# DeltaNet and mixture of depths on one core: the state's chain ahead in the plan, W's second copy in W's own form, a smaller first G, five elimination steps by columns

## The chip, the core and the metric

The kernel runs on one core of one Trainium2 chip. The metric is the time of one execution on the device in microseconds; three runs of the kernel before gave 325.86 us in the median (323.55 to 333.23).

## What is computed

Four batches, eight heads, 768 tokens, 48 channels a head. First a delta rule over the tokens, one state of 48x48 for each batch and head:

```python
k_n = k / (norm(k) + 1e-6)
for t in range(S):
    y[:, :, t] = einsum('bhd,bhde->bhe', q[:, :, t], state)
    v_old = einsum('bhde,bhd->bhe', state, k_n[:, :, t])
    state = state + beta_t * einsum('bhd,bhe->bhde', k_n[:, :, t], v_t - v_old)
```

Then, with x the heads' outputs side by side (4, 768, 384), a mixture of depths: each token's score is x times w_gate; the 128 tokens of the highest score in each batch go through `relu(x @ w1) @ w2` (384 to 1024 to 384), scaled by the sigmoid of the score, and are added to x; the other tokens keep x.

## The kernel before

**Chunks, blocks and the state.** The tokens are cut in chunks of 64 (`C`), 12 for each of two groups of two batches, so `NU` is 24 chunks, called i. Four chunks make a block e (`BC`), six in all. In a chunk the delta rule is a triangular system, which is solved ahead of the recurrence for all heads and halves of 32 tokens at once:

- `prep(i)` loads k and q, transposes them on PE (`turn`, L401; copies at L414), makes G, the products of k with k (`products`, L460; the first block by `first_products`, L450, in pieces of 32 rows; copy at L466), and the products of q with k (L460; masked by DVE at L473). From block 1 on, G goes to DRAM (`spill`, L470) and comes back turned (`turn_in`, L535), so that each partition holds one 32x32 matrix.
- `eliminate(e)` inverts those matrices on DVE, one per partition: the diagonal (L541), its root on ACT (L545), the scales (L549 to L554), the scaling (L570), then the steps j = 1 to 30. A step is a product of a column with a row into `tmp` (L593), the next row by itself (L579), and an addition (L599); the last steps go row by row (L579). `final` is L604. In blocks 2 to 4 (`over`) the table is then written to DRAM (`out_a`, L611) and read back turned (`back`, L617) as `tt`; in the other blocks DVE turns it (L607), and `tt` is read from `g`. `join` makes Z (L681) of the two halves.
- `recur(i)` is the recurrence. In order: R, keys times the old state (`mm_r`, L735), copied on ACT (L745); W, the table times the values (`mm_w`: L766, or L772 where `direct`), with a second copy of its lower half in another bank (L779); W's copy on ACT (L795 or L798 and L800); M, which joins the halves (`mm_m`, L790); its copy to `wbd` (L805); S, the product that adds to the state in PSUM (`mm_s`, L816); its copies (L823). The state's chain is R, W, M, S and their copies. Off it lie Q and P, the outputs (`mm_q` L833, `mm_p` L845, copy L851), the score (DVE, L863), and the values' scaling for the next chunk (`vh`, L709), which waits for the copy of R, as both use a bank.
- `ranking(g)` counts for each token the scores above its own (L939 to L980), and `depths(b)` takes the chosen tokens by an indirect DMA, runs the two layers (L1067, L1083) and writes the rows back.

**What sets the order.** Nothing is looped on the chip: `Plan` orders all operations on the host. Each has an engine, a cost, dependences, a latency, a priority (smaller goes first) and the rings of buffers it takes and gives. `pick` takes, for an engine that is free, the operations that can start earliest, and among these the smallest priority; one that would delay a `hard` one by more than 0.2 is left out unless its priority is as small. Where PE would wait in the plan, `fill` puts matmuls of constants (`filler`, L305). So costs and priorities act on the chip through the order alone: each engine, and SP's queue of DMAs, then runs its list in order.

```python
u = 10 * i            # recur: all of the chain, Q and P at u + 3
u = 40 * e - 100 + i % BC   # prep: keys and G of block e
u = 10 * i - 30       # join: Z
```

Priorities in prep for q's transposes are 10i - 20, and for the products of q with k 10i - 14.

**PSUM.** Eight banks: two pairs (`pair`), two single ones (`one`), two for the state (`psta`). `constants` writes the banks once by matmuls on ones (L341), of each pair only the second bank.

Of the kernel before, what the change touches and what calls it, by code (L numbers as in the profile page):

```python
# [16 lines left out]
C = 64  # L17
HC = 32
# [139 lines left out]
def kernel(  # L158
# [47 lines left out]
    def ring(name, count, shape, dt=FP32):  # L206
        rings[name] = [sbuf(f"{name}{m}", shape, dt) for m in range(count)]
        plan.ring(name, count)
# [23 lines left out]
    ring("zt", 3, [GI, HC])  # L232
    ring("tt", 2, [NB, C])
    ring("x", 2, [2, DM])
# [88 lines left out]
    def constants():  # L323
# [4 lines left out]
        for t in rings["q"] + rings["k"][BC:]:  # L328
            nc.gpsimd.memset(t[:, :, D:], 0.0)
        for t in rings["tt"]:  # L330
            nc.gpsimd.memset(t, 0.0)
# [7 lines left out]

        for t in [*psta, *[t[:, 1] for t in rings["pair"]]]:  # L340
            nc.tensor.matmul(t, lhsT=warm[:, :P], rhs=warm, start=True, stop=True)  # L341
# [77 lines left out]
    def prep(i):  # L419
# [21 lines left out]
        def first_products():  # L441
            kt, ps = got("kt", i), banks(kb)
            for x in range(GI):
                h4, par = divmod(x, 2)
                for bb, rt in four:
                    k_of = kt[half[rt], bb * 2 + h4]
                    for out, rows, tok, cols in ((slice(0, C), hi[bb], hi[par], half[par]),
                                                 (slice(HC, C), lo[bb], lo[par], lo[par]),
                                                 (slice(0, HC), lo[bb], lo[par], hi[par])):
                        nc.tensor.matmul(ps[rows, rt, x, out], lhsT=k_of[:, tok],  # L450
                                         rhs=k_of[:, cols], start=True, stop=True)
# [54 lines left out]
        if first:  # L506
            n["g"] = pe(1.0, first_products, n["ek"], u, take=gt, work=1024, hard=True)
            n["eg"] = [act(0.59, out_g, [n["g"]], u, give=[kb], hard=True)]
        else:
            n["g"] = pe(0.52, products("kt", kb), [*n["ek"], N[e * BC].get("g")], u, take=gt,  # L510
                        work=1024, lat=LATE["g"])
            n["eg"] = [act(0.48, out_g, [n["g"]], u, give=[kb])]
            n["sg"] = sp(0.6, spill, n["eg"], u, take=[("gd", e)] * (i % BC == 0), lat=4.6)
            n["sg"].own = 4.2
        v = 10 * i - 14
        n["w"] = pe(0.58, products("qt", kw), n["eq"] + n["ek"] + [N.get(("end", 0))], v,
                    work=1024, take=[kw, ("p", i)], lat=LATE["p"])
        n["ep"] = [dve(0.62, out_p, [n["w"]], v - 200, give=[kw])]

    def eliminate(e):  # L520
# [23 lines left out]
        def root():  # L544
            nc.scalar.activation(nrm[:, 0], nrm[:, 0], AF.Sqrt)  # L545

        def scales():
            nn, b = nrm[:, 1], bh[e % 2]
            nc.vector.tensor_scalar(out=nn, in0=nrm[:, 0], scalar1=1e-6, scalar2=-1.0,  # L549
                                    op0=ALU.add, op1=ALU.mult)  # L550
            nc.vector.reciprocal(b, nn)
            nc.vector.scalar_tensor_tensor(out=b, in0=b, scalar=-1.0, in1=b,
                                           op0=ALU.mult, op1=ALU.mult)
            nc.vector.tensor_tensor(out=b, in0=b, in1=bt[:, e], op=ALU.mult)  # L554

# [19 lines left out]
        def row(i, j):  # L575
            a = got("a", e)
            to, of = (a[:, :j, i], a[:, :j, j]) if over else (a[:, i, :j], a[:, j, :j])
            by = a[:, j, i:i + 1] if over else a[:, i, j:j + 1]
            nc.vector.scalar_tensor_tensor(out=to, in0=of, scalar=by, in1=to,  # L579
                                           op0=ALU.mult, op1=ALU.add)  # L580
# [47 lines left out]
        s["in"] = dve(0.2, diag, [ti, N.get(("nrm", e - 1)), N.get(("late", e - 1))], u, **hard)  # L628
        s["rt"] = act(0.25, root, [s["in"]], u - 1, hard=True)
        s["sc"] = dve(1.0, scales, [s["rt"], *N["beta", e]], u, **hard)  # L630
        N["nrm", e] = s["nt"] = dve(0.2, turn_n, [s["sc"]], u + 2)
# [3 lines left out]
        nxt, rest = last, [last]  # L635
        for j in range(1, HC - 1):
            if j >= HC - 4:
# [25 lines left out]
    def join(e, m, direct):  # L663
# [20 lines left out]
        def ez():  # L684
            nc.scalar.copy(got("zt", i), view())

        n["bk"] = [s["to"]] if direct else s["bk"]
        n["z"] = pe(0.3, z, n["bk"], u, work=128, take=[key, ("zt", i)],
                    give=[] if direct else [("g", e)], **hard)
        n["ez"] = [act(0.17, ez, [n["z"]], u, give=[key], **hard)]  # L690
# [3 lines left out]
    def values(i, after):  # L694
# [4 lines left out]
        def vh():  # L699
# [5 lines left out]
            for h in range(2):  # L705
# [6 lines left out]
                     take=[("v", i)], lat=5.0 if i < 2 else LATE["v"])  # L712
        n["vh"] = dve(0.68 if c > 0 else 0.5, vh, [n["lv"], N["e", e]["nt"], *after],
                      10 * i - 60 if c == 0 else 10 * i - 400)

    def recur(i):
# [4 lines left out]
        n, o = N[i], R.get(i - 1, {})  # L721
        r = R[i] = {}
        wb, s_old, s_new = wbd[i % 2], sts[(i + 1) % 2], sts[i % 2]
        kw, ky = ("pair", i, "W"), ("one", i, "Y")
# [30 lines left out]
        def mm_w(h4):  # L755
            def emit():
                x, again = got("v", i), got(*kw)[:, 1, GI * D:2 * GI * D].rearrange(
                    "p (r d) -> p r d", d=D)
                direct = n["direct"]
                t = got("g" if direct else "tt", e)  # L760
                for y in range(2 * h4, 2 * h4 + 2):
                    for bb, par in four:
# [7 lines left out]
                        else:  # L770
                            for rows in (lo, hi):
# [3 lines left out]
                                                 stop=False, skip_group_check=True)  # L775
                    for par in range(0 if direct else 2):
                        a = 2 * y + par
                        xa = a if c == 0 else y // 2 * 4 + par * 2 + y % 2
                        nc.tensor.matmul(again[hi[par], y], lhsT=t[half[1], ch * GP + a, :HC],  # L779
                                         rhs=x[half[1], xa], start=False, stop=True,  # L780
                                         skip_group_check=True)
            return emit


# [88 lines left out]
        if c > 0:  # L873
            r["r"] = [pe(0.38, mm_r(h4), [*o["es"][h4], *o["w"], x], u, work=768, **hard)
                      for h4 in range(2)]
            r["xr"] = xs = [act(0.22, out_r(h4), [r["r"][h4]], u, **hard) for h4 in range(2)]
        if i + 1 < NU:
# [17 lines left out]
        for h4 in range(2):  # L895
            r["mw"].append(pe(0.33 if n["direct"] else 0.37, mm_w(h4),
                              [xs[h4 % len(xs)], *n["bk"], *o.get("w", []), *r["mw"]], u,
                              give=[("v", i)] + [("tt", e)] * (e > 0) + [("g", e)] * n["direct"],
                              take=[kw] if h4 == 0 else [], work=384, **hard))
        e1 = act(1.0 if n["direct"] else 0.38, out_w1, [*r["mw"], o.get("mm")], u, **hard)  # L900
        r["mm"] = pe(0.47, mm_m, [e1, *n["ez"]], u, give=[("zt", i)], work=192, **hard)
        r["w"] = [act(0.47, out_w(par), [r["mm"], prev2.get("p"), *prev2.get("s", [])], u,
                      give=[kw], **hard) for par in range(2)]
        if not late:
            r["s"] = [pe(0.36, mm_s(h4), [*r["w"], *sum(o.get("es", []), []),
                                          *sum(prev2.get("es", []), []), clear, N.get("zero")],
                         u, work=768, **hard) for h4 in range(2)]
            r["es"] = [[act(0.32, out_s(h4, rt), [r["s"][h4], o.get("q"), *o.get("r", [])], u, **hard)
                        for rt in range(2)] for h4 in range(2)]
# [3 lines left out]
        if c > 0:  # L913
            r["q"] = pdep = pe(0.68, mm_q, [*sum(o["es"], []), *n["eq"], *r["w"]], u + 3,
                                 take=[ky], work=768)
        r["p"] = pe(0.76, mm_p, [*qdep, *n["ep"], pdep], u + 3, work=1536,
                    take=[] if c > 0 else [ky], give=[("kt", i), ("qt", i), ("p", i)],
# [5 lines left out]
    def ranking(g):  # L923
# [4 lines left out]
        def stage(j0, j1, prev):  # L928
# [50 lines left out]
            def add():  # L979
# [5 lines left out]
            a0 = act(0.3 * w, spot, sc + prev[2:], u, take=[key] + [("rep", g)] * (j0 == 0), **hd)  # L985
            m0 = pe(0.25, spread, [a0], u, take=[kr], give=[key],
                    lat=LATE["rep"] if g == 0 else 0.22, **hd)
            a1 = act(0.17, out_rep, [m0], u, give=[kr], lat=LATE["above"] if g == 0 else 0.12, **hd)
            d = []
            for j in range(j0, j1):  # L990
                d.append(dve(0.2 * (1 + (j > 0)) + 0.067 * (j + 1), above(j), [a1] + d[-1:],
                             u + 1, take=[km] if j == j0 else [],
                             give=[("rep", g)] if last else [], **hd))
            m1 = pe(0.03 * w * (j1 + j0) + 0.1, sums, d + prev[1:2], u + 1, take=[kc], give=[km],
                    lat=LATE["sums"] if g == 0 else 0.22, **hd)
# [183 lines left out]
```

## Time and profile before

| | |
|---|---|
| three runs, median (lowest to highest) | 325.86 us (323.55 to 333.23) |
| the profiled execution | 327.94 us |
| its span, first to last instruction | 326.2 us |
| mean granted clock of TensorE | 0.988 |
| PE busy, of it L305 (198 of 251 are in the trace) | 296.0 us, 57.3 us |
| weight loads, DVE, ACT, POOL busy | 217.1, 218.6, 151.3, 27.8 us |
| steps of the eliminations L593, L599, L579 (DVE) | 55.4, 52.2, 45.5 us |
| W and its second copy, L766 and L779 (PE) | 24.5, 20.5 us |
| DMA over all queues | 37.07 MB |

Busy time is a share of the span of about 326 us; the time of an execution is 1.7 us more than its span here. PE's matmuls overlap in the records, so a mean duration (239 ns for L766) is not their spacing: that is read from the starts in the timeline. A row of the timeline has start, length, engine, line, operation and count, and in brackets how long the engine had been idle and what ended that. SPq is SyncE's queue that issues DMAs.

### The profile page before, as it was taken

How to read it: one execution, taken by the hardware profiler on the slowest of the kernel's cores; microseconds unless marked ns; L12 is line 12 of the kernel's file. 1: busy time of each engine (PE TensorE's matmuls, PEld its weight loads, DVE VectorE, ACT ScalarE, POOL GpSimd, SP SyncE). 2: the span in 40 equal slices, each digit the busy share in tenths (PEclk: the TensorE clock that was granted, in tenths of full speed). 3: DMA queues.
4: the chain of work that ended last, by engine and by line, in shares of the span. 5: the costliest groups of instructions: out<-in, count | busy, mean ns of one | idle time of the engine just before them, and what ended most of it. 6: DMA issues, size and time to landing. Idle time of an engine off the chain costs nothing.

```text
span 326.2 us, 17293 instructions
## 1 busy us (share of the span) xinstructions
PE 296.0 (91%) x7598; PEld 217.1 (67%) x7651; DVE 218.6 (67%) x861; ACT 151.3 (46%) x399; POOL 27.8 (9%) x51
## 2 busy tenths in 40 slices
PE   7689989999969999899989999999988999999993
PEld 3455547778556677577677777688766788576571
DVE  6179999999849599969897699885644413512000
ACT  2335327677434556265643656355567454111110
POOL 8120002001000020001000110000020000031011
PEclk9999999999996999999999999999999999999999
DMA  6896977643878558896759584425231011120000
GB/s 99 160 148 143 237 156 137 153 101 59 217 171 167 168 148 159 169 193 176 175 130 212 139 154 86 101 53 110 40 91 32 4 50 28 27 73 26 2 26 24
DMA packets 127547, 37.07 MB, mean 114 GB/s; under 512 B 119536, under 2 KB 123760, under 8 KB 127472
## 3 DMA queue, kind: packets, MB, share of 16 engines
q1 hardware_dynamic: 119904, 33.13, 47.1%
q10 hardware_dynamic: 7056, 1.26, 2.4%
q0 software_dynamic: 512, 1.57, 1.5%
q8 instruction: 60, 0.98, 1.2%
q14 instruction: 15, 0.12, 0.1%
HBM read 22.58 MB, written 12.32 MB: 107 GB/s over the span
## 4 chain that ended last, share of the span: by engine, by line
PE 66%; DVE 8%; issue 8%; ACT 8%; DMA 4%; SPq 2%; ACTq 1%; POOLq 0%; another core or an unknown queue 0%; DVEq 0%
PE one L305 8%; PE pair L460 6%; PE pair L766 5%; PE pair L1067 5%; PE one L1083 5%; PE psta L816 5%; PE pair L779 4%; PE one L845 4%; PE psta L735 4%; PE one L833 4%; PE pair L401 4%; PE pair L790 3%; PE pair L681 2%; DMA gd<-g 2%; DVE tmp L593 2%
## 5 line engine op out<-in xcount | busy, mean ns | idle before, releaser
L305 PE MATMUL one<-warm 128*128 128x512 bf16 x198 | 57.3, 389 | 7.1 <-issue 5.6
L593 DVE TENSOR_TENSOR tmp<-a 128x29 f32<-128x29 f32 (+8 forms) x162 | 55.4, 342 | 0.0
L599 DVE TENSOR_TENSOR a<-a,tmp 128x29 f32<-128x29 f32 (+8 forms) x162 | 52.2, 322 | 0.0
L579 DVE SCALAR_TENSOR_TENSOR a<-a 128x28 f32<-128x28 f32 (+29 forms) x198 | 45.5, 238 | 0.1
L305 PEld LDWEIGHTS <-warm 128*128 128x128 bf16 x251 | 19.9, 99 | 20.5 <-issue 3.3
L823 ACT COPY s<-psta 64x192 f32<-64x192 f32 x88 | 27.6, 314 | 11.8 <-PE psta L816 9.2
L709 DVE TENSOR_TENSOR psta<-v,nnT 128x192 f32<-128x192 f32 x44 | 14.7, 362 | 20.9 <-ACT v L745 20.9
L805 ACT COPY wbd<-pair 64x384 f32<-64x384 f32 x48 | 22.7, 473 | 12.0 <-PE pair L790 11.5
L562 POOL TENSOR_SCALAR_AFFINE_SELECT mb<-bh 128x1024 f32<-128x1024 f32 x6 | 11.6, 1926 | 167.9 <-DVE bh L554 142.0
L766 PE MATMUL pair<-v,tt 64*64 64x48 f32 x576 | 24.5, 239 | 1.3 <-issue 0.5
L1067 PE MATMUL pair<-xeT,w_sb 128*64 128x128 f32 x384 | 23.5, 275 | 2.2 <-ACT hT L1074 2.2
L795 ACT COPY w<-pair 128x384 f32<-128x384 f32 x18 | 8.6, 479 | 33.9 <-PE pair L779 25.9
L1067 PEld LDWEIGHTS pair<-xeT,w_sb 128*64 128x64 f32 x384 | 21.0, 137 | 4.3 <-ACT hT L1074 2.9
L959 DVE TENSOR_SCALAR_CACHE_REDUCE mk<-rep 128x64 bf16<-128x64 f32 (+10 forms) x22 | 13.4, 610 | 14.4 <-ACT rep L952 14.4
L1083 PE MATMUL one<-w_sb,hT 128*64 128x384 f32 x128 | 22.4, 490 | 0.0
L779 PE MATMUL pair<-v,tt 64*32 64x48 f32 x288 | 20.5, 219 | 0.7 <-issue 0.7
L766 PEld LDWEIGHTS pair<-v,tt 64*64 64x64 f32 x576 | 15.6, 135 | 8.0 <-ACT qt L414 1.2
L845 PE MATMUL one<-wbd,p 128*64 128x96 f32 x384 | 20.3, 247 | 0.0
L745 ACT COPY v<-psta 128x192 f32<-128x192 f32 x44 | 14.0, 328 | 13.2 <-PE psta L735 12.9
L816 PE MATMUL psta<-wbd,k 128*64 128x96 f32 x352 | 19.8, 253 | 0.2
L833 PE MATMUL one<-s,qt 128*64 128x96 f32 x352 | 18.9, 247 | 0.7 <-issue 0.7
L466 ACT COPY g<-pair 128x512 f32<-128x512 f32 x24 | 14.0, 588 | 11.8 <-PE pair L450 5.1
(119 smaller groups left out, 482.1 us busy)
## 6 DMA issues: line engine op xcount, KB each, us to landing
gd<-g SPq DMA_DIRECT2D x20, 256.0 KB
q<-in_q_dram SPq DMA_DIRECT2D x48, 96.0 KB
v<-in_v_dram SPq DMA_DIRECT2D x48, 96.0 KB
out_dram<-x SPq DMA_DIRECT2D x20, 192.0 KB
k<-in_k_dram SPq DMA_DIRECT2D x36, 96.0 KB
a<-gd SPq DMA_DIRECT2D x20, 128.0 KB
w_sb<-in_moe_w_dram SPq DMA_DIRECT2D x3, 512.0 KB
ad<-a SPq DMA_DIRECT2D x3, 512.0 KB
```

The source lines that it names most:

```text
L305: nc.tensor.matmul(to if name == "one" else to[:, 0], lhsT=warm[:, :P], rhs=warm, start=True, stop=True)
L579: nc.vector.scalar_tensor_tensor(out=to, in0=of, scalar=by, in1=to, op0=ALU.mult, op1=ALU.add)
L593: nc.vector.tensor_tensor(out=view(), op=ALU.mult, in0=x[0].to_broadcast(shape), in1=x[1].to_broadcast(shape))
L599: nc.vector.tensor_tensor(out=to, in0=to, in1=view(), op=ALU.add)
L766: nc.tensor.matmul(w_of(bb)[half[par], y], lhsT=t[half[bb], ch * GP + a], rhs=x[half[bb], xa], start=(y == 0), stop=False, skip_group_chec ...
L779: nc.tensor.matmul(again[hi[par], y], lhsT=t[half[1], ch * GP + a, :HC], rhs=x[half[1], xa], start=False, stop=True, skip_group_check=True)
L816: nc.tensor.matmul(psta[h4][half[rt], bb * 2 * D:(bb + 1) * 2 * D], lhsT=t[:, a], rhs=wb[:, a].rearrange("p h d -> p (h d)"), start=False, ...
L823: nc.scalar.copy(s_new[half[rt], :, rt].rearrange("p (b h x) d -> p b h x d", b=2, h=2)[:, :, h4], psta[h4][half[rt], :GI * D].rearrange(" ...
L833: nc.tensor.matmul(got(*ky)[half[bb], :2 * GI * D] .rearrange("p (h r x d) -> p h x r d", h=2, r=2, x=2)[:, h4, par], lhsT=got("qt", i)[:, ...
L845: nc.tensor.matmul(py[half[bb], x * 2 * D:(x + 1) * 2 * D], lhsT=t[:, a], rhs=wb[:, a].rearrange("p h d -> p (h d)"), start=(c == 0 and x ...
L1067: nc.tensor.matmul(ps[half[x]], lhsT=w1_sb[:, t, c0:c0 + C], rhs=got("xeT", b)[:, t], start=(t == 0), stop=(t == KD - 1))
L1083: nc.tensor.matmul(got("one", b, "o")[c0:c1, :DM], lhsT=got("hT", b)[:, f, c0:c1], rhs=w2_sb[:, f], start=(f == 0), stop=(f == KF - 1))
```

## The change

- In `recur`, R, W, M, S and their copies get the priority `uc = u - 35` in place of u; Q, P, the output and the score keep theirs.
- W's second copy was made in pieces of 32 columns among the matmuls of `mm_w`. Now `mm_again` makes it after both halves of `mm_w`, by matmuls with 64 columns of weights. `tt` has 32 columns of zeros ahead for this (`tts`), and each weight begins 32 columns earlier: the upper half of the output takes what nobody reads. Z gives `tt` back too.
- `first_products` leaves out a third of its matmuls, a block that nobody reads; so that its bank isn't read unwritten, `constants` writes both banks of each pair.
- The steps j = 1 to 5 go by `column`: for each c < j one instruction that adds column j times an element to column c; 15 instructions in place of 15 (five each of L593, L579, L599).
- The negated root comes from ACT (`root` has two instructions), and `scales` has three instructions for four.
- Costs in the plan: g 0.52 to 0.6 and 1.0 to 0.85, w 0.58 to 0.62, z 0.3 to 0.36, vh 0.68 to 0.58, and small ones of the outputs and the ranking.

```diff
-    ring("tt", 2, [NB, C])
+    tts = [sbuf(f"tt{m}", [HC + NB * C]) for m in range(2)]
+    rings["tt"] = [t[:, HC:].rearrange("p (n t) -> p n t", t=C) for t in tts]
+    plan.ring("tt", 2)
...
-        for t in [*psta, *[t[:, 1] for t in rings["pair"]]]:
+        for t in [*psta, *[t[:, x] for t in rings["pair"] for x in range(2)]]:
...
                     for out, rows, tok, cols in ((slice(0, C), hi[bb], hi[par], half[par]),
-                                                 (slice(HC, C), lo[bb], lo[par], lo[par]),
-                                                 (slice(0, HC), lo[bb], lo[par], hi[par])):
+                                                 (slice(HC, C), lo[bb], lo[par], lo[par])):
...
             nc.scalar.activation(nrm[:, 0], nrm[:, 0], AF.Sqrt)
+            nc.scalar.activation(nrm[:, 1], nrm[:, 0], AF.Copy, scale=-1.0, bias=-1e-6)
...
             nn, b = nrm[:, 1], bh[e % 2]
-            nc.vector.tensor_scalar(out=nn, in0=nrm[:, 0], scalar1=1e-6, scalar2=-1.0,
-                                    op0=ALU.add, op1=ALU.mult)
-            nc.vector.reciprocal(b, nn)
-            nc.vector.scalar_tensor_tensor(out=b, in0=b, scalar=-1.0, in1=b,
+            nc.vector.scalar_tensor_tensor(out=b, in0=nn, scalar=-1.0, in1=nn,
                                            op0=ALU.mult, op1=ALU.mult)
+            nc.vector.reciprocal(b, b)
...
+        def column(j, c):
+            a = got("a", e)
+            to, of = (a[:, c, j + 1:], a[:, j, j + 1:]) if over else (a[:, j + 1:, c], a[:, j + 1:, j])
+            by = a[:, c, j:j + 1] if over else a[:, j, c:c + 1]
+            nc.vector.scalar_tensor_tensor(out=to, in0=of, scalar=by, in1=to,
+                                           op0=ALU.mult, op1=ALU.add)
...
-        for j in range(1, HC - 1):
+        few = 5
+        cols, before = {}, []
+        for j in range(1, few + 1):
+            for c in range(j):
+                cols[c] = dve(0.075 + 1.04e-3 * (HC - 1 - j), (lambda j=j, c=c: column(j, c)),
+                              [last, *([cols[c]] if c < j - 1 else before)], u, **hard)
+            before = list(cols.values())
+        nxt = x = dve(0.0, lambda: None, [*cols.values()], u, **hard)
+        rest = [x]
+        for j in range(few + 1, HC - 1):
...
+        uc = u - 35
...
-                    for par in range(0 if direct else 2):
-                        a = 2 * y + par
-                        xa = a if c == 0 else y // 2 * 4 + par * 2 + y % 2
-                        nc.tensor.matmul(again[hi[par], y], lhsT=t[half[1], ch * GP + a, :HC],
-                                         rhs=x[half[1], xa], start=False, stop=True,
-                                         skip_group_check=True)
...
+        def mm_again():
+            x, t = got("v", i), tts[plan.live["tt", e][1]]
+            ps = got(*kw)[:, 1, GI * D:2 * GI * D].rearrange("p (r d) -> p r d", d=D)
+            for a in range(GP):
+                y, par = divmod(a, 2)
+                xa = a if c == 0 else y // 2 * 4 + par * 2 + y % 2
+                n0 = (ch * GP + a) * C
+                nc.tensor.matmul(ps[half[par], y], lhsT=t[half[1], n0:n0 + C],
+                                 rhs=x[half[1], xa], start=False, stop=True,
+                                 skip_group_check=True)
...
+        if not n["direct"]:
+            r["mw"].append(pe(0.3, mm_again, r["mw"][-1:], uc, give=[("v", i), ("tt", e)],
+                              work=192, **hard))
```

## Prediction

> **What bounds the kernel now.** I read the page, then the timeline of one chunk of the recurrence, then of one hand-over between VectorE's elimination and that recurrence, then the waits.
>
> ```profile
> PE 296.0 (91%) x7598; PEld 217.1 (67%) x7651; DVE 218.6 (67%) x861; ACT 151.3 (46%) x399; POOL 27.8 (9%) x51
> ...
> PE   7689989999969999899989999999988999999993
> ...
> DVE  6179999999849599969897699885644413512000
> ACT  2335327677434556265643656355567454111110
> ...
> PEclk9999999999996999999999999999999999999999
> ...
> L305 PE MATMUL one<-warm 128*128 128x512 bf16 x198 | 57.3, 389 | 7.1 <-issue 5.6 <-ACT xeT L1058 1.0
> ```
>
> PE at 91% isn't PE as the limit: L305 is filler on constants, put where the plan sees PE wait. From 25 to 220 us DVE is as full as PE: six eliminations stand there in a row. So three things must be told apart: PE's work, the chain of the state through PE and ACT, and the eliminations. PE's timeline of chunk 8 to chunk 9, between two products of the state (L816):
>
> ```profile
> 138.81 0.88 PE L816 MATMUL psta<-wbd,k 128*64 128x96 f32 x16
> ...
> 140.84 0.83 PE L735 MATMUL psta<-s,w_sb 128*64 128x96 f32 x16
> ...
> 142.00 0.33 PE L766 MATMUL pair<-v,tt 64*64 64x48 f32 x8
> 142.26 0.28 PE L779 MATMUL pair<-v,tt 64*32 64x48 f32 x4
> 142.47 0.33 PE L766 MATMUL pair<-v,tt 64*64 64x48 f32 x8
> ...
> 143.87 0.82 PE L305 MATMUL one<-warm 128*128 128x512 bf16 x2
> 144.62 0.54 PE L790 MATMUL pair<-w,zt 32*32 32x48 f32 x32
> ...
> 145.49 0.82 PE L305 MATMUL one<-warm 128*128 128x512 bf16 x3
> 146.24 0.88 PE L816 MATMUL psta<-wbd,k 128*64 128x96 f32 x16
> ```
>
> This chunk takes 7.43 us (138.81 to 146.24), all of it chain: product, copy of the state, R (L735), copy, W (L766 with L779, 1.87 us to 143.87), copy, M (L790), copy. The fills stand in front of waits for ACT, so they cost little here. Other chunks of the recurrence take 8.0 to 9.5 us (L816 starts at 184.51, 192.85, 201.58, 211.56, 219.67, 227.71, 237.18): 0.6 to 2 us of other work stands in the chain.
>
> The hand-over of elimination 2, DVE's and SP's timelines:
>
> ```profile
> 110.86 1.22 DVE L604 TENSOR_TENSOR a<-a,mb 128x1024 f32<-128x1024 f32 x1
> 113.99 0.18 DVE L549 TENSOR_SCALAR nrm<-nrm 128x32 f32<-128x32 f32 x1 [1.90 <-ACT nrm L545]
> ...
> 118.99 1.51 SPq L611 DMA_DIRECT2D ad<-a  x1
> ...
> 123.45 3.78 SPq L617 DMA_DIRECT2D tt<-ad  x4
> ```
>
> It ends at 112.08, its table leaves SP only at 118.99 (behind a spill at 118.33) and Z reads it at 130.4, 18.4 us later; chunk 8 starts on it. The next two take 18.8 and 21.4 us. Meanwhile DVE waits for the chain, in its own order:
>
> ```profile
> DVE psta L709 <- ACT v L745: 20.9, 15, 4.0
> ...
> 74.90:112.10 37.20, 32.97 (x880) 23.98 (x878) 29.16 (x116) 17.62 (x46) 1.28 (x1) 0.91 0.76 171
> ...
> 96.60:103.40 6.80, 6.47 (x101) 3.95 (x99) 6.57 (x28) 2.65 (x7) 0.00 (x0) 0.50 0.89 153
> ```
>
> (The last two are windows; after DVE, ACT and POOL comes the granted clock.) Elimination 2 has 8 us of idle DVE in 37.2. PE was busy for 4.68 us of 89.0:96.6, in wait for tt, and then had clock 0.50 for 6.8 us. So the chain and the eliminations hold each other up, through queues in order.
>
> **The change, part by part.** The orders of both programs tell what moves.
>
> *W's second copy.* Eight groups alternate: 8 matmuls of 64*64 in 0.26 us, 4 of 64*32 in 0.21. L460, 64*64 alone with 64 columns, runs 32 in 0.62, 19.5 ns each; at that price 8 take 0.156, which leaves 0.10 for the switch; then L779's four take 0.11, 26 ns each. The Trainium skill, "TensorEngine Tiling (Array Packing)", Key Properties, says that a change of tiling mode drains TensorE; the row agrees, some 0.1 us a switch. Now 32 matmuls run at 19.5 ns (0.62), then 16 of 64*64 for the copy. Those all read the rows half[1]. "TensorE: Matmul & The Clock Gate", Part 3, speaks against this: a weight load overlaps running matmuls only where the row group differs, and a load takes columns/1.2 GHz. That is 53 + 22 = 75 ns each, 1.2 us for 16, W 1.85: nothing gained. But L816 and L735 load 64 columns onto all rows, time after time, at 41 ns each (16 in 0.66), so the load hides in this trace. I take 26 to 45 ns, 0.42 to 0.72 us, middle 0.5: W 1.15 for 1.87, 0.7 saved in each of 18 chunks: 13 us of PE, and of chain where nothing else is late.
>
> *The chain ahead.* Fills: 93 to 92 ahead of the first L816, 158 to 76 behind it; 82 at 0.207 (L305's spacing) are 17 us of PE, but only the part that overshot its wait counts. The 0.6 to 2 us of other work in each chain should fall to about 0.5: a chunk takes 7.43 - 0.7 + 0.5, and 0.1 for slip, so 7.4 us, where it waits for no elimination. PE's own work from chunk 13 to 22, added in the order of after with the rows' prices, is 65 us for ten chunks, 6.5 each: PE isn't the limit there.
>
> *First G.* 96 matmuls in 1.22 us become 64, 0.4 saved in each of four chunks; of the two issue gaps between them (0.74, 1.83) a third, with a third of the instructions. Against that two more fills of a bank ahead of the first transpose, 0.5 us each (L341), with no idle time ahead of that transpose: they count. -1.6 - 0.9 + 1.0 = -1.5 (-3 to +0.5).
>
> *Columns.* Five steps by three instructions took 2.1 us (51.85 to 53.95, start to start); now 15 of L579's kind on 26 to 30 columns, 0.16 to 0.18 apart in the last rows of each elimination: 2.4 to 2.7. Loses 0.3 to 0.6 in each of six. *Scales*: one instruction of 0.18 goes from DVE to ACT at L545's 0.23: nothing, as DVE waits for ACT there (1.90 above). tt's longer hold (Z gives it back too) ends long before the ring comes round: nothing; if not, SP's write of the table is late. The changed costs act through the order alone.
>
> *SP.* out_a of elimination 2 now stands ahead of all four spills of block 4 (before, behind three); the reads of tt stand behind three of them, and out_a of elimination 4 behind the four reads of a for block 5, which need the last spill, and so chunk 12. Behind those wait out_a, then tt, Z and W of chunk 16: 3 us, as much as before (177.7 to 181.25).
>
> **The sum, in the profiled execution's time** (span 326.2, run 327.9).
> - Elimination 0 ends 1.5 earlier, 1 too late with its columns: about 44.5; 1 at 76 (77.8), with fewer stalls; 2 at 111 (112.1): its 21.9 of own work after the scaling, 6.8 of other DVE work, 2 idle in place of 8, but it starts behind elimination 1's transpose.
> - Table of 2 at 127, 16 us later: out_a 5 earlier in its queue, then three spills. L816 of chunk 8 follows W by 4: 131 (was 138.8).
> - Chunks 9, 10 and 11 at 7.4 end at 153. Elimination 3: 29.6 of DVE, ends 141; table 17 later, 158; L816 of 12 at 162 (176.4).
> - Elimination 4 ends 170, table 187; chunks 13 to 15 reach W of 16 at 187.5: both together; L816 of 16 at 191.6 (211.6).
> - Block 5's last G is copied at 165 and its a is read by 177 (12 us later; 15.6 before), then 39 us of DVE: 216 (221.5). Chunks 17 to 19 reach 214; chunk 20 waits 2, and 2 for ranking and an ACT table load there: 224 (249.5). Chunk 21 waits for tt, 10.5 after 216: 231.5. Chunk 22: 239 (266.1).
> - Behind it PE is full in both, 60.1 us to the end. After has 0.7 less W and more left over: P 0.66, a transpose 0.4, a product 0.65, turn_x 0.25, 36 fewer matmuls of L1067 done early at 59 ns, 2.1: 63.5. Span 302.5.
> - Clock: the fills are gone from the waits for tt of chunks 5, 16 and 21. The page on the clock gate ("Why this matters for your kernels") warns of PE idle for over some 3 us; here 2.9 idle in 7.6 gave 6.8 at half clock. One window costs about 3 us (half of 6.8); I count one more: 305.5, run 307. Against the median of the runs (325.86; the profiled run is 0.6% over it) that is 305 to 307; I say 306.
>
> **Rivals.**
> 1. *As summed*, 306. For it: the cleared 0.7 of W, and the idle DVE and the slip of chunks that the trace shows. 65%.
> 2. *The copy's loads don't hide*: W stays at 1.85. Chunks take 8.0; 16 at 197, 22 at 248, tail 64.5: 314. Against it: 41 ns on L816. 12%.
> 3. *Queues in order*: chunks run ahead, then wait in PE, with Q, P and next G behind them; DVE waits on L709 as before, G of block 5 is late. 0.9 us more in each of 22 chunks, no change: 325. For it: 20.9 us of L709. 8%.
> 4. *Clock, partly*: four more windows at half clock, 318. 8%.
> 5. *Clock, slower than before*: without fills PE idles over 3 us in each wait for a table and in gaps of chunks; from eight more windows (8 x 3 = 24 us against the gain of 21) it is slower: twelve give 306 + 36 - 3 = 339. Against it: within chunks gaps for ACT are about 1 us, and 34 fills stand at chunk 8, the longest wait. 7%.
>
> **How the numbers follow.** The likeliest is 306; its own range is 298 (chunks at 7.0, tables 2 us sooner each) to 313 (elimination handed over as late as before). To leave out no more than 2 in 10 it reaches to rivals 2 and 4: 297 to 321. Over 2% (about what the measurement can tell; 319.3): faster 65 + 12 + 6 = 83%; within 2%: 2 of rival 4, 8 of rival 3: 10%; slower 7%.
>
> **What would show it.** Right: W in one piece of 1.0 to 1.3 us; L816 starts 7.0 to 7.8 apart; L709's wait under 12 us; chunk 8 at 127 to 134, chunk 22 before 245; at most two dips of the clock. Wrong: the copy over 1 us; eliminations 2 to 4 no earlier than 112, 146 and 178; block 5's read of a past 182; three or more dips; a tail over 66 us.

## The result, and the profile after

Four runs of the changed kernel gave 316.58 us in the median (314.0 to 318.14), four of the kernel before on the same chip 325.67 (323.55 to 333.23): a ratio of 0.9716 [0.9655, 0.9778]. That is 9.1 us less, where 20 were forecast; the time lies inside the forecast's range. Medians, here and below, are of all runs of a kernel, ratios of those runs that lie within 1.5% of its fastest. The profiled execution of the changed kernel took 314.0 us with a span of 312.3 (before: 327.9 and 326.2), so the sum of the forecast, 305.5, is to be held against 312.3.

The page of the kernel after:

```profile
PE 271.9 (87%) x7409; PEld 205.7 (66%) x7442; DVE 220.8 (71%) x855; ACT 152.8 (49%) x405; POOL 28.2 (9%) x51
...
DVE  6379989987999999918999759999754524502000
...
PEclk9999999999999999969999999999999999999999
...
L307 PE MATMUL one<-warm 128*128 128x512 bf16 x135 | 39.3, 392 | 4.7 <-issue 4.5
```

PE is busy for 24 us less, of which the filler on constants (L307, L305 before) makes 18. The clock has one dip in the middle, as before: half clock from 131.8 to 138.6. W in a chunk in which nothing stood between, from PE's timeline:

```profile
195.55 0.70 PE L783 MATMUL pair<-v,tt 64*64 64x48 f32 x32
196.06 0.66 PE L804 MATMUL pair<-v,tt 64*64 64x48 f32 x16
196.64 0.88 PE L869 MATMUL one<-wbd,p 128*64 128x96 f32 x16
```

32 matmuls of W, then 16 of its copy (L804), and P (L869) begins 1.09 us after W did. The copy's sixteen start 27 to 29 ns apart in the mean, in 15 of the 18 chunks that have one: what was 1.87 us is about 1.1.

Where the forecast goes wrong can be seen at the first hand-over. SP's timeline around the table of elimination 2, which DVE finished at 110.7:

```profile
107.49 1.53 SPq L372 DMA_DIRECT2D w_sb<-in_moe_w_dram  x1
113.51 1.52 SPq L393 DMA_DIRECT2D q<-in_q_dram  x2
...
121.09 0.57 SPq L619 DMA_DIRECT2D ad<-a  x1
...
126.65 4.08 SPq L625 DMA_DIRECT2D tt<-ad  x4
```

SP issues nothing from 109.0 to 113.5, then ten DMAs in 7.6 us, then the table (L619), and later its way back (L625). PE's timeline at the other end:

```profile
131.57 0.28 PE L783 MATMUL pair<-v,tt 64*64 64x48 f32 x2 [2.74 <-DMA tt<-ad]
132.97 1.10 PE L783 MATMUL pair<-v,tt 64*64 64x48 f32 x30 [1.12 <-DMA tt<-ad]
```

W of chunk 8 waits for `tt`, and S of chunk 8 starts at 139.0, as late as before (138.8), though chunk 7 had its S at 106.7 (before 125.3). The waits of DVE and of SP's queue (in total, times, longest):

```profile
DVE psta L727 <- ACT v L764: 15.8, 13, 7.6
...
SPq L393 <- DMA bt<-in_beta_dram: 4.4, 1, 4.4
```

DVE's longest wait for the chain grew from 4.0 to 7.6 us: it stands at 134.1, where chunk 8 is late, and holds elimination 3. SP's 4.4 us are the hole from 109.0: a load of q stands in wait for a load of beta, which it doesn't read. In the program's waits every DMA issued by SP or ACT waits for the landing of the earlier one that used the same of eight completion semaphores, and these are handed round in program order over both queues. Here the semaphore that SP waits for reached its count at 113.4, with the landing of a beta load that ACT issued at 111.5. The beta loads are issued by ACT, behind `root` of the next elimination, so SP waits for ACT.

Two windows of the kernel after, elimination 2 from end to end and the stretch behind S of chunk 22 (PE, PEld, DVE, ACT, POOL, clock):

```profile
77.00:110.70 33.70, 31.57 (x1039) 26.14 (x1042) 32.68 (x130) 22.71 (x65) 2.25 (x1) 1.00 0.68 144
246.40:312.30 65.90, 57.38 (x927) 41.58 (x924) 16.32 (x56) 14.02 (x36) 5.84 (x6) 1.00 0.11 32
```

DVE is idle for 1.0 us in elimination 2, where it was 8 of 37.2. The tail is 65.9 us for 60.1. Where the 927 matmuls come from is in the groups of that window:

```profile
L1094 PE MATMUL pair<-xeT,w_sb 128*64 128x128 f32 x384 | 23.1, 274 | 2.9 <-ACT hT L1101 2.9
...
L869 PE MATMUL one<-wbd,p 128*64 128x96 f32 x48 | 2.6, 250 | 0.0
```

Before, 352 of the first product with w1 and 32 of P lay behind chunk 22.

PE's time in three kinds (the union of its matmul records in order of start; all other than L305/L307 is "work"): before, 241.1 us of work, 54.9 of fills, 30.2 idle; after, 234.5, 37.3 and 40.4. So 17.6 us of fills went, 10 came back as idle time, and the work fell by only 6.6, though W alone gave up some 13.

### The profile page after: what moved, and what is told of

Its sections match the earlier page's. It is cut to its first block, busy times and chain, and to the rows that moved or that the text cites. A ratio compares the mean times of both kernels' runs of the same rounds, so it can differ in the third digit from the quotient of the medians.

```text
span 312.3 us, 16891 instructions
## 1 busy us (share of the span) xinstructions
PE 271.9 (87%) x7409; PEld 205.7 (66%) x7442; DVE 220.8 (71%) x855; ACT 152.8 (49%) x405; POOL 28.2 (9%) x51
## 4 chain that ended last, share of the span: by engine, by line
PE 51%; DVE 15%; DMA 11%; issue 9%; ACT 9%; SPq 3%; ACTq 1%; POOLq 0%; DVEq 0%
PE one L307 5%; PE pair L461 4%; PE one L869 4%; PE one L857 4%; PE pair L1094 4%; PE psta L840 3%; PE one L1110 3%; PE pair L814 3%; PE psta L754 3%; PE pair L783 3%; PE pair L403 3%; DMA out_dram<-xe,idx 3%; DVE tmp L601 2%; ACT s L847 2%; DVE a L607 2%
## 5 line engine op out<-in xcount | busy, mean ns | idle before, releaser
L601 DVE TENSOR_TENSOR tmp<-a 128x144 f32<-128x144 f32 (+12 forms) x132 | 46.6, 353 | 0.1
L607 DVE TENSOR_TENSOR a<-a,tmp 128x144 f32<-128x144 f32 (+12 forms) x132 | 46.7, 353 | 0.0
L307 PE MATMUL one<-warm 128*128 128x512 bf16 x135 | 39.3, 392 | 4.7 <-issue 4.5
L579 DVE SCALAR_TENSOR_TENSOR a<-a 128x28 f32<-128x28 f32 (+24 forms) x168 | 40.7, 251 | 0.2
L829 ACT COPY wbd<-pair 64x384 f32<-64x384 f32 x48 | 22.7, 473 | 17.1 <-PE pair L814 16.8
L562 POOL TENSOR_SCALAR_AFFINE_SELECT mb<-bh 128x1024 f32<-128x1024 f32 x6 | 11.9, 1990 | 170.4 <-DVE bh L554 105.7
L727 DVE TENSOR_TENSOR psta<-v,nnT 128x192 f32<-128x192 f32 x44 | 15.1, 376 | 16.1 <-ACT v L764 15.8
L307 PEld LDWEIGHTS <-warm 128*128 128x128 bf16 x168 | 13.8, 100 | 14.5 <-issue 2.5
L869 PE MATMUL one<-wbd,p 128*64 128x96 f32 x384 | 21.9, 251 | 1.4 <-issue 1.4
L416 ACT COPY qt<-pair 128x512 f32<-128x512 f32 x24 | 14.0, 591 | 18.1 <-PE pair L403 15.2
L587 DVE SCALAR_TENSOR_TENSOR a<-a 128x26 f32<-128x26 f32 (+4 forms) x90 | 19.4, 287 | 0.1
L869 PEld LDWEIGHTS one<-wbd,p 128*64 128x64 f32 x384 | 17.3, 136 | 3.0 <-issue 1.8
L819 ACT COPY w<-pair 128x384 f32<-128x384 f32 x18 | 8.6, 479 | 21.0 <-PE pair L804 19.6
L1101 ACT ACTIVATE hT<-pair 128x512 f32<-128x512 f32 x8 | 4.8, 597 | 28.7 <-PE pair L1094 28.7
L783 PE MATMUL pair<-v,tt 64*64 64x48 f32 x576 | 14.5, 228 | 5.0 <-DMA tt<-ad 3.9
```

The lines of the kernel that those rows point to most:

```text
L307: nc.tensor.matmul(to if name == "one" else to[:, 0], lhsT=warm[:, :P], rhs=warm, start=True, stop=True)
L601: nc.vector.tensor_tensor(out=view(), op=ALU.mult, in0=x[0].to_broadcast(shape), in1=x[1].to_broadcast(shape))
L607: nc.vector.tensor_tensor(out=to, in0=to, in1=view(), op=ALU.add)
L783: nc.tensor.matmul(w_of(bb)[half[par], y], lhsT=t[half[bb], ch * GP + a], rhs=x[half[bb], xa], start=(y == 0), stop=False, skip_group_chec ...
L829: nc.scalar.copy(wb[half[par], :, par].rearrange("p (b r) d -> p b r d", b=2), x.rearrange("p (b x) -> p b x", b=2)[:, :, :GI * D] .rearra ...
L869: nc.tensor.matmul(py[half[bb], x * 2 * D:(x + 1) * 2 * D], lhsT=t[:, a], rhs=wb[:, a].rearrange("p h d -> p (h d)"), start=(c == 0 and x ...
```

## The experiments

The median of the runs, that of the kernel before on the same chip, and the ratio. Different chips differ by 2 us and more, so rows are compared by their ratio or on one chip (A, B, C). Where no ratio stands, the runs of the kernel were too far apart for one, and the range is given.

| kernel | chip | us | before | ratio [95%] |
|---|---|---|---|---|
| change, out_a and tt on GpSimd's queue | A | 320.26 | 330.22 | 0.9742 [0.9615, 0.987] |
| change without the chain ahead | A | 323.59 | 330.22 | 0.985 [0.9771, 0.9929] |
| change with the old copy of W | A | 332.39 | 330.22 | 1.0065 [1.0013, 1.0116] |
| change without columns | A | 319.04 | 330.22 | 0.9684 [0.9586, 0.9783] |
| change again | B | 322.18 | 330.77 | 0.9816 [0.9669, 0.9963] |
| change, beta on GpSimd's queue | B | 314.48 | 330.77 | 0.9608 [0.9509, 0.9707] |
| change, beta, out_a and tt there | B | 317.13 | 330.77 | 0.9694 [0.956, 0.9829] |
| before + W's copy | B | 322.33 | 330.77 | none (314.22 to 325.07) |
| change, beta there, again | C | 315.18 | 327.84 | 0.9636 [0.9566, 0.9706] |
| the same, without columns | C | 315.31 | 327.84 | 0.9644 [0.9572, 0.9715] |
| before + W's copy + beta there | C | 314.33 | 327.84 | 0.9605 [0.9545, 0.9665] |
| before + the chain ahead | C | 335.80 | 327.84 | 1.0287 [1.0195, 1.0379] |

**The table alone on another queue.**

```diff
-            nc.sync.dma_start(out=ad[e % 2], in_=got("a", e))
+            nc.gpsimd.dma_start(out=ad[e % 2], in_=got("a", e))
...
-                    nc.sync.dma_start(out=got("tt", e)[rows, :, hf * HC:(hf + 1) * HC],
+                    nc.gpsimd.dma_start(out=got("tt", e)[rows, :, hf * HC:(hf + 1) * HC],
```

> The changed kernel, with the table's way out (out_a) and back (the reads of tt) issued from GpSimd's queue in place of SyncE's; the order of all else stays. Theory 1 (the missing 8 us are lost at chunk 8, since out_a stood in SyncE's queue from 110.7 to 121.1): out_a leaves within 2 us of the end of elimination 2, tt lands by 122, and chunk 8's product of the state starts 3 to 6 us earlier than 139.05 (PE's own order has transposes ahead of it that wait for DVE until 128); 3 to 7 us less in all, 310 to 313. Theory 2 (the chunks themselves are slow, the table only seems late): chunk 8 moves by 3 at most, and the end by less than 1.5. Theory 3: the copies of 128-byte rows take longer from GpSimd's queue (over 10 us), and it is slower.

The table's way back was now issued at 120.2 to 122.5, some 7 us sooner (126.7 to 130.2 above), and chunk 8 came at 139.7, no sooner. SP stood from 104.8 to 115.0 in wait for a beta load, so a load of q was late (issued at 127.4 to 129.3), and PE's list has the transpose of that q ahead of W of chunk 8 (it waited 4.1 us, to 131.6). The late table alone is not the cause; SP's hole is ahead of both.

**The chain back in its place.**

```diff
-        uc = u - 35
+        uc = u
```

> The changed kernel, with the chain's priority back at 10i. Theory of the forecast (a chunk loses its 0.6 to 2 us of other work): chunks are 8 us again in the mean from 16 to 22, some 6 us slower there, and as the plan then fills PE differently ahead of the blocks, 320 to 326 in all. Rival (the form of W's copy brings all of the gain): 315 to 318, no different from the changed kernel.

323.59 us: chunk 8 at 139.1, chunk 22 at 262.3, the tail 59.5. On this chip it lies above the two kernels with the chain ahead and the new copy (319.04 and 320.26), by 3 to 5 us, at a lower granted clock too (0.963 to 0.972; theirs is 0.970 to 0.987 but for one run). The runs on chip C don't confirm that the order is worth it.

**W's copy back in its old form.**

```diff
+                    for par in range(0 if direct else 2):
+                        a = 2 * y + par
+                        xa = a if c == 0 else y // 2 * 4 + par * 2 + y % 2
+                        nc.tensor.matmul(again[hi[par], y], lhsT=t[half[1], ch * GP + a, :HC],
+                                         rhs=x[half[1], xa], start=False, stop=True,
+                                         skip_group_check=True)
...
-            r["mw"].append(pe(0.3, mm_again, r["mw"][-1:], uc, give=[("v", i), ("tt", e)],
-                              work=192, **hard))
```

> The changed kernel, with W's second copy back in pieces of 32 columns among W's matmuls. By the row (1.9 for 1.15 us in each of 18 chunks): 0.75 us in the 10 to 11 chunks whose pace is the chain's own, the rest hidden in waits for a table: 6 to 10 us slower, 322 to 327. If all 18 count: 13 us, 330. Rival (the eliminations on DVE and their hand-over set the pace everywhere): under 3 us slower.

332.39 us: all of the gain and some 2 us more are gone. PE's work is 249.9 us, the tail 70.0.

**No step by columns.**

```diff
-        few = 5
+        few = 0
...
-        nxt = x = dve(0.0, lambda: None, [*cols.values()], u, **hard)
-        rest = [x]
+        nxt, rest = last, [last]
```

> The changed kernel, with the first five steps of each elimination back as product, row and sum; the scales stay as changed. By the rows the columns lose 0.3 to 0.6 us in each of six eliminations; where eliminations set the pace (2 to 4) this is 1 to 2 us faster, 314.5 to 316. Rival (columns gain, since they have fewer dependences): 1 to 3 us slower. As the plan reorders with it, up to 2 us either way have no such cause.

Chunk 8 comes at 135.1 for 139.0, elimination 3 ends at 138.2 for 147.8, and chunk 22 stands at 251.2 for 246.4: DVE gains up to 10 us, which don't reach the end. The ratio can't be told from the change's.

**The change again, as the control of the next three.**

> The changed kernel itself, as the measure for the three beside it on the same chip: a ratio of 0.972 to before again (0.966 to 0.978).

On this chip it was slower: 322.18, with SP in wait for beta loads three times, 10.3 us in all, and chunk 8 at 142.7.

**The beta loads of blocks 1 to 5 on GpSimd's queue.** They then use completion semaphores of that queue's own, none of the eight; PE's and SP's lists stay as they are.

```diff
-            betas(e, act, nc.scalar, [N["e", e - 1]["rt"]], 40 * e - 82)
+            betas(e, act, nc.gpsimd, [N["e", e - 1]["rt"]], 40 * e - 82)
```

> The changed kernel, with beta's small loads of blocks 1 to 5 issued from GpSimd's queue in place of ScalarE's; the plan, PE's list and SyncE's list stay the same. Theory 4 (a load in SyncE's queue waits for the landing of the DMA that had the same completion semaphore before it; where this is a beta load, SyncE waits for ScalarE, which comes to it only after the root of the next elimination): SyncE no longer stands from 109.0 to 113.5, the table of block 2 leaves at about 116.5 in place of 121.1, the q loads that PE's transposes wait for come as much earlier, and chunk 8's product of the state is at 134 to 136 (139.05); from there all is 3 to 5 us earlier: 3 to 6 us less than the changed kernel. Rival (SyncE's issue time of 0.6 us a DMA, or DVE's masks that PE's transposes wait for, hold chunk 8 in any case): under 1.5 us.

314.48 (313.4 to 315.3), which is 7.7 us under the control on the same chip (319.1 to 324.9): more than forecast. SP's timeline in the second run of this kernel, for the stretch shown above:

```profile
107.07 1.58 SPq L393 DMA_DIRECT2D q<-in_q_dram  x2
...
115.44 0.57 SPq L619 DMA_DIRECT2D ad<-a  x1
...
121.86 3.95 SPq L625 DMA_DIRECT2D tt<-ad  x4
```

The hole is gone, and the table leaves at 115.4 and its way back at 121.9, each some 5 us sooner. The control on chip B shows it in pairs: the table leaves at 117.4 for 124.8, chunk 8 comes at 137.1 for 142.7, chunk 22 at 247.2 for 255.0, and the span is 313.6 for 320.6. So the wait of one queue for a load of another is shown, and that it costs; up to 3.4 us of the 7 in this pair are the clock's, as the control had 17.0 us at half clock ahead of chunk 22 and this run 10.2.

**Both on GpSimd's queue.**

> The changed kernel, with both beta's loads and the table's way out and back on GpSimd's queue. Theory 4: the table lands at about 120 to 122, but PE's transposes of q stand ahead of W in its list and wait for loads in SyncE's queue, so chunk 8 is at 131 to 135, 4 to 8 us less than the changed kernel, 0 to 3 less than with beta alone. Rival (DVE's masks hold it): no less than with beta alone.

317.13: no better than the beta loads alone.

**The kernel before with W's copy in W's form and nothing else** (`tts`, `mm_again` and the banks that it needs, at priority u).

> The kernel before, with nothing changed but W's second copy (64 columns, after both halves of W) and what it needs. By the row, 0.75 us in each of 18 chunks, of which those behind a table's wait are hidden: 6 to 10 us less than before (ratio 0.97 to 0.98). If the gain needs the chain's new priority: under 3 us. If DVE's eliminations set the pace: under 3 us as well, with their ends where they were.

322.33 beside the change's 322.18. But the five runs reach from 314.22, at a granted clock of 1.000, to 325.07, at 0.970: W's form alone isn't told apart from the whole change.

**A control for the last three.**

> A second run of the changed kernel with the beta loads of blocks 1 to 5 on GpSimd's queue, as the control for the next three on the same chip. Expected: 313 to 317 us, 3 to 5% under the kernel before.

315.18. Chunk 8 at 133.8, chunk 22 at 246.4, span 312.9.

**Beta loads on GpSimd's queue and no columns** (both edits above).

> The changed kernel with the beta loads on GpSimd's queue and with no step by columns (few = 0): the five steps go as before, by L593, L599 and L579's kind. If the columns cost what the forecast said (0.3 to 0.6 us in each elimination) and the eliminations set the time of the recurrence, it is 1 to 3 us below its control; if the eliminations are covered by PE, or if the columns cost nothing, the two are within 1 us.

315.31, the same as the control. Yet eliminations 1 to 5 end at 73.0, 108.7, 133.6, 166.9 and 213.5, where the control has 78.2, 113.3, 143.0, 175.9 and 217.0. Up to 9 us of DVE's time come to nothing at the end. In part the order of PE's list takes them: M of chunk 14 starts 9.0 us after W (168.9, 177.9), as the ranking, passed to and fro between PE, ACT and DVE, stands ahead of that chunk's Z; in the control it is 1.7 us.

**W's copy and the beta loads in the kernel before**, the chain not ahead.

> The kernel before with only two edits: W's second copy in W's form, and the beta loads of blocks 1 to 5 on GpSimd's queue. The state's chain is not ahead. Theory A (the chain ahead is worth something once SP no longer stands on a beta load): 318 to 322, 3 to 6 us above the control. Theory B (W's form is all, the order gives back in the tail what it gains in the recurrence): 313 to 317, within 2 us of the control.

314.33: two edits, without the order, the first G, the scales or the columns, do what the whole change and the beta edit do together. Its chunk 22 comes at 251.5, five us after the control's, and its tail is 60.6 us for 66.5. PE's timeline of this kernel, from S of chunk 16 on:

```profile
203.61 0.88 PE L821 MATMUL psta<-wbd,k 128*64 128x96 f32 x16
204.32 0.83 PE L838 MATMUL one<-s,qt 128*64 128x96 f32 x16
204.98 0.83 PE L850 MATMUL one<-wbd,p 128*64 128x96 f32 x16
205.64 0.83 PE L737 MATMUL psta<-s,kt 128*64 128x96 f32 x16
```

and of the changed kernel at the same place:

```profile
199.29 0.88 PE L857 MATMUL one<-s,qt 128*64 128x96 f32 x16
200.15 0.88 PE L840 MATMUL psta<-wbd,k 128*64 128x96 f32 x16
200.96 1.03 PE L461 MATMUL pair<-qt,kt 64*64 64x64 f32 x32
201.92 0.55 PE L754 MATMUL psta<-s,kt 128*64 128x96 f32 x8
202.40 0.45 PE L699 MATMUL pair<-tt,g 32*32 32x32 f32 x32
202.78 0.55 PE L754 MATMUL psta<-s,kt 128*64 128x96 f32 x8
...
204.59 1.16 PE L869 MATMUL one<-wbd,p 128*64 128x96 f32 x16
```

In the first, S, Q, P and R, all of tiles of 128*64, follow one another 0.66 to 0.71 us apart. In the second, R is made in two halves with a product in 32*32 between them, and products of other tiles stand ahead of R and of P: R takes 0.48 + 0.48 us, S 0.81, P 1.09.

**The chain ahead in the kernel before, and nothing else.**

> The kernel before with the priority of the state's chain alone (uc = u - 35); W's second copy stays in pieces of 32 columns. Theory A (order and W's form each bring part of the gain): 319 to 324. Theory B (W's form is all of it; the order alone frees nothing, as PE then meets the late tables sooner): 324 to 333, as the kernel before or slower, and the tail behind chunk 22 over 65 us.

335.80, slower than before by 2.9%, and above what either theory gave. The waits of SP's queue in it:

```profile
SPq L391 <- DMA bt<-in_beta_dram: 15.0, 1, 15.0
SPq L470 <- DMA bt<-in_beta_dram: 7.5, 1, 7.5
SPq L611 <- DMA bt<-in_beta_dram: 3.1, 1, 3.1
```

25.6 us in these three; before, such waits made 14.9. Elimination 2 ends 5 us later than before, chunk 8 stands at 151.4, 12.6 later; chunk 22 is level with before (266.1), and the tail is 67.6 us for 60.1. So by the marks the tail holds all of the loss of this span (333.7 for 326.2).

## Why the prediction was right and wrong

**Right: W's copy.** The trace has 27 to 29 ns for a matmul of the copy, at the low end of the 26 to 45 taken, and W in one piece of 1.1 us. The rule of the Trainium skill that was weighed against it ("TensorE: Matmul & The Clock Gate", Part 3: a load overlaps only where the row group differs; with the load time from "LDWEIGHTS (loading the stationary operand)" of that page an estimate of 75 ns each) doesn't hold for these loads: the sixteen all use the same rows. Each goes to the other half of the columns from the one before it; whether that is why, no run here shows. The 13 us forecast for it are 13.5 in the kernel before together with the beta loads' move (327.84 to 314.33), 8.4 without that, by medians of runs up to 11 us apart, and 8 to 11.5 by the run with the old copy, from the difference of its ratio to the change's two.

**Wrong: the step "The chain ahead".** Its own share of the forecast follows by subtraction, if the parts add up: the profiled run was to fall by 20.9; W -13, first G -1.5, columns +2.7 and a clock window +3 leave -12 for the order with its tail. Measured, the order is worth +8.0 alone, and nothing when the copy is new and the beta loads are out of the way (315.18 with it, 314.33 without, along with the small parts). Two things failed in that step.

1. *The hand-over of elimination 2*, the part headed SP: "Table of 2 at 127". The landing that let W go on was at 133.0, 6 us late; from W to S it took 6.1 us for the 4 forecast, with the clock at half until 138.6. The forecast counted which DMAs stand ahead of out_a in SP's list, but neither that ten of them at 0.76 us each stand behind a hole, nor that a load in that list can wait for ACT's queue through a completion semaphore. It put these waits at nothing, though SP's waits in the kernel before show them:

```profile
SPq L391 <- DMA bt<-in_beta_dram: 12.9, 4, 7.7
SPq L611 <- DMA bt<-in_beta_dram: 2.0, 1, 2.0
```

The marks (the start of S, and of the tail) show how the 8 us go through to the end; the last three columns are of chip C:

| mark, us | forecast | change | with beta moved | and no columns | before + W + beta |
|---|---|---|---|---|---|
| elimination 2 ends | 111 | 110.7 | 113.3 | 108.7 | 108.6 |
| S of chunk 8 | 131 | 139.0 | 133.8 | 129.9 | 135.1 |
| elimination 3 ends | 141 | 147.8 | 143.0 | 133.6 | 141.2 |
| S of 12 | 162 | 168.7 | 167.5 | 156.4 | 171.4 |
| S of 16 | 191.6 | 200.1 | 199.0 | 194.2 | 203.6 |
| S of 22 | 239 | 246.4 | 246.4 | 244.0 | 251.5 |
| tail | 63.5 | 65.9 | 66.5 | 66.5 | 60.6 |
| span | 302.5 (+3) | 312.3 | 312.9 | 310.5 | 312.1 |

Held against the marks, the miss of the profiled run is +8.0 at chunk 8, -0.6 from there to chunk 22, +2.4 in the tail, and -3.0 for the clock window that this run didn't have: 6.8.

2. *PE isn't the limit there.* In the profiled run's marks this doesn't show: from chunk 8 to chunk 22 it took 107.4 us for the 108 forecast. But PE's price for the order was wrong, and with it what the order is worth. The forecast had "PE's own work from chunk 13 to 22 ... 6.5 each: PE isn't the limit there", 65 us in all; the trace has 70.0. From chunk 16 to 22 it has 43.3 us of work, 0.4 of fills and 2.6 idle in 46.2 us: 7.2 of work a chunk, and little left to close. So mending the first mark alone doesn't bring the 306. Four kernels with the chain ahead had no dip of the clock between chunk 8 and chunk 22: the change, those with beta moved and with beta and the table moved on chip B, and the one without columns on chip C. Their chunk 8 comes at 139.0, 137.1, 135.6 and 129.9, their chunk 22 at 246.4, 247.2, 247.7 and 244.0. (The column "with beta moved" had 10.2 us at half clock in between.) Of the lead of 9 us at chunk 8, 2.4 are left at chunk 22; a nearly full PE is seen from chunk 16 on, and at chunk 14 it was the order of PE's list, as said above.

The rows' prices were those of the order before, where products of one tile form stand in rows. The order breaks these rows. PE's time in the groups R, Q and P, and its changes of tile form between neighbours, those to and from tiles of 128*128, the form of the fills, left out:

| kernel | R | Q | P | changes |
|---|---|---|---|---|
| before | 17.6 | 15.4 | 16.5 | 281 |
| before + W + beta | 17.0 | 15.3 | 17.1 | 153 |
| change without the chain ahead | 18.4 | 15.1 | 17.0 | 154 |
| before + the chain ahead | 21.0 | 16.9 | 18.6 | 321 |
| change with the old copy | 21.3 | 17.6 | 20.0 | 323 |
| change | 21.2 | 16.8 | 19.6 | 202 |

Each kernel with the chain ahead spends 56.5 to 58.9 us on the three, each without it 49.4 to 50.5, for the same matmuls. The clock isn't why: two kernels with no dip but in their last 3 us, the one with beta moved and no columns, which has the order, and before + W + beta, which hasn't, have 57.1 and 49.4. In the kernel after, a matmul of 128*64 starts 54 ns after one of its form in the mean, 133 after one of 64*64, and one of 64*64 starts 199 after one of 128*64 (gaps of 0.4 us and more left out): about 0.1 us a change, as the Trainium skill says in kind ("TensorEngine Tiling (Array Packing)", Key Properties: a change of the tiling mode drains TensorE). The 40 to 49 changes that the order adds are then 4 to 5 of the 7 to 8 us; where the rest lies stays open. The forecast used this rule for W and not for the order. Thus the order hands PE about as much as it saves by starting earlier: on chip C the chain leads by 5 us at chunk 22 and is caught in the tail. In its tail the change has as much of S, R and W as the kernel before, and on top 32 matmuls with w1 (1.7 us), 16 of P (0.9), 42 of the ranking (1.5), a product (0.7), a transpose (0.5) and three turns of x (0.5). The forecast's list of these had all but the ranking.

That the runs with the order are longer on R, Q and P is measured; that the changes of form are why is read from the traces, and no run here kept the order and put the rows together again. What the order alone loses in the kernel before is not settled either: SP's 25.6 us, the longer tail and a lower granted clock (0.951 to 0.969, its control 0.975 to 0.992) all stand in these runs, and the order with the beta loads moved and the old copy was not run.

**The small parts.** The columns cost about what the upper end of 0.3 to 0.6 us says. In elimination 1, where in both kernels no other work of DVE stands between, it is 3.64 us from the first column to the next step (49.74 to 53.38), where five steps took 3.00 (50.95 to 53.95). The forecast's 2.1 began at 51.85, behind the first instruction, which takes 0.98 us before and 1.00 after, both beside GpSimd's mask (L562, to 51.90 and to 50.69); with no mask beside it, in elimination 3 of the kernel after, it takes 0.21. The other columns start 0.15 to 0.19 apart, as forecast, where nothing else comes between. Their cost doesn't show in the time: without them, and with beta moved, it is 315.31 for 315.18. Elimination 0 ended at 45.1 (44.5 forecast, 45.7 before); block 5's a was read from 176.4 (177) and elimination 5 ended at 218.0 (216). DVE's wait L709, to be under 12 us, is 15.8.

**The rivals.** The second (the copy's loads don't hide) is out by its own row, though its 314 lies near. The third (queues in order) is right in kind at one place, SP and DVE at chunk 8. The fourth is right in part: by their granted clock (0.989, 0.968, 0.975, 0.973; a window at half clock is 6.8 us) the four runs of the changed kernel had 1.0, 3.0, 2.3 and 2.5 windows and took 314.0, 317.3, 315.9 and 318.1 us, so that the median lies 2.6 above the profiled run. The run with the fewest windows is the shortest, but among the other three 2.5 took longer than 3.0, and no run took the windows away. The fifth didn't come.

**The best version** is the kernel before with two edits, W's copy in W's form and the beta loads on GpSimd's queue: 314.33 (314.12 to 314.76), 0.9605 [0.9545, 0.9665] of before. The whole change with the beta loads moved isn't told apart from it.

## What to carry to other kernels

An order that puts a chain first is paid in the resource that the chain shares: count what it costs that engine (changes of tile form, rows broken up), not only whose wait it shortens, and use prices from the order that will stand. Look at which engine is full behind the point where the gain arises; a lead that meets a full engine, or other work ahead in its list, is given back, in part or in whole. In a queue, count the issues at their own price, and follow each wait to its semaphore, in the profile before the change already: a load can stand behind another queue's load that it has nothing to do with.

## What the hardware showed beyond that

- A DMA on SP waited up to 15.0 us for a beta load on ACT's queue that it shares only a completion semaphore with; the same loads on GpSimd's queue left no such wait.
- A DMA issued by SP takes about 0.6 us of its queue in the median, and ten in a row made 7.6 us of lateness.
- Weights of 64*64 on one and the same row group, to one half of the columns and the other in turn, loaded anew for each matmul of 48 columns, ran 27 to 29 ns apart.
- An instruction of DVE's elimination that starts beside GpSimd's mask took 0.98 to 1.01 us and ended within 0.1 us of it; without one beside it the same took 0.15 to 0.24.
